# Loading q in runs of eight tokens, with the last tokens late, loads planned behind the transposes, and q @ kv joined with the next kv

## Chip, cores and metric

The kernel runs on one core of one Trainium2 chip. The metric is the device time of one execution in microseconds. A run counts as slow if it lies more than 1.5% above the fastest of the same kernel. Medians and ranges below are of all runs; ratios, intervals and verdicts (faster, same or slower at 2%, or unclear) are of fast runs. The sessions ran on several chips, so each kernel is compared with runs of the kernel before in the same session.

## The reference

A linear attention over 8 batches feeds a SoLU layer with a LayerNorm; B = 8, H = 8, S = 576, D = 64, d_model = 512, d_ff = 1024.

```python
kv  = np.einsum('bhsd,bhse->bhde', k, v)
o   = np.einsum('bhsd,bhde->bhse', q, kv)
x   = o / np.sqrt(np.mean(o * o, -1, keepdims=True) + 1e-6) * g_norm   # then to (B*S, H*D)
h   = x @ w_in
u   = h * softmax(h, -1)
ln  = (u - mean(u)) / np.sqrt(var(u) + 1e-6) * g_ln
out = ln @ w_out                                                      # (4608, 512), float32
```

## The kernel before

The tokens are worked off in nine chunks of 512. Chunks 0 to 7 are the first 512 tokens of each batch; the ninth holds the last 64 tokens of all eight. A small list scheduler (`Plan.order`) fixes the order of the pieces on each engine from estimated lengths. The output leaves in 36 tiles of 128 rows by 512 columns, four per chunk, with four output buffers (`ob`). GpSimd issues the loads; the SP queue issues most stores, and the DMA transposes of q for chunks 4 to 8.

```python
XBAR = tuple(range(4, NC))               # chunks whose q is transposed by DMA; NC = 9
bufs = {"k": 3, "v": 3, "q": 3, "qT": 3, ... "ob": 4}
q_last = big.tile([128, H, 4, D], BF16, name="q_last")
# ...
def load_q(b, hs):                       # 4 tokens in a run: 512 B packets after the cast to bf16
    nc.gpsimd.dma_start(
        T["q", b].rearrange("p h j d -> p h (j d)")[:, hs],
        q[b, :, 0:512, :].rearrange("h (p j) d -> p h (j d)", j=4)[:, hs])
# ...
def q_turn(c):
    t = T["qT", c] = tile_of(("qT", c), [128, H, 2, 128], BF16)
    nc.sync.dma_start_transpose(
        t.rearrange("q h y p -> q (h y) p"), T["q", c].rearrange("p h j d -> p (h j d)"))
# ...
def o_mm(c, hf, tag):                    # q @ kv; the last chunk takes every eighth column of each batch
    ...
            for b in [c] if c < B else range(B):
                cols = slice(0, 128) if c < B else slice(b, 128, B)
# ...
def store(c, m):
    j = 2 * (m % 2) + m // 2
    if c < B:                            # DRAM side: 128 rows x 512
        dst = out[c * S:c * S + 512, :].rearrange("(p j) d -> j p d", j=4)
    else:                                # DRAM side: 16 x 8 x 512
        dst = out.rearrange("(b s) d -> b s d", b=B)[:, 512:S, :].rearrange("b (p j) d -> j p b d", j=4)
    (nc.scalar if c == NC - 1 and m % 2 else nc.sync).dma_start(dst[j], T["ob", c, m][:, :])
```

The softmax here doesn't subtract the row's maximum and nothing guards it: scores larger than these inputs give would overflow.

## Time and profile before

| | before |
|---|---|
| time, median (range) | 197.0 us (196.5 to 197.7), 3 runs |
| span of the profiled run (whose own time is 195.0 us) | 193.1 us |
| TensorE busy | 179.8 us, 93% |
| a store of 256 KB, issue to landing | 2.9 us (median) |
| bytes stored | 9.44 MB |

The page's main lines are in the prediction below. Two of its other parts matter here: the chain of work that ended last (shares of the span by engine, then by line) and the DMA issues (count, KB each, us to landing).

```profile
PE 64%; DMA 20%; ACT 7%; POOL 4%; DVE 2%; issue 2%; SPq 0%; POOLq 0%; DVEq 0%; ACTq 0%
...
out_dram<-ob_sb SPq DMA_DIRECT2D x34, 256.0 KB, 2.9
```

The end is set by TensorE.

### The profile page before, as it was taken

The numbers are of one execution on the slowest core, as the hardware profiler recorded it, in microseconds if no ns is written. First come the engines' busy times: TensorE is split into PE (matmuls) and PEld (weight loads), VectorE is DVE, ScalarE is ACT, GpSimd is POOL, SyncE is SP. The second block draws the span as 40 slices with busy tenths as digits, with TensorE's granted clock in tenths as the row PEclk, the third lists the DMA queues.
The fourth block names the chain that finished last, engine by engine and source line by source line (L and its number), as shares of the span: only waits on it lengthen the run. The fifth ranks groups of instructions, "written<-read, shape, count | busy, mean of one in ns | idle before, by whom it ended". The sixth has DMA issues, their size and how long they took to land.

```text
span 193.1 us, 5442 instructions
## 1 busy us (share of the span) xinstructions
PE 179.8 (93%) x2282; PEld 88.3 (46%) x2282; DVE 122.6 (63%) x241; ACT 141.0 (73%) x245; POOL 127.9 (66%) x136
## 2 busy tenths in 40 slices
PE   7897997898899998999899999999999999999991
PEld 2352454553354643544354435445445554544460
DVE  1456588468684887496477658567575747666450
ACT  2038888869895997799689987989789496655520
POOL 7981799500999987977499776568285838846200
PEclk9999999999999999999999999999999999999999
DMA  1999999999996999899999996363111111211206
GB/s 22 204 204 266 357 203 205 206 224 248 233 201 86 147 190 258 113 185 168 292 214 200 212 111 182 108 116 114 54 54 58 58 54 58 109 58 54 110 7 213
DMA packets 36040, 29.71 MB, mean 154 GB/s; under 512 B 11816, under 2 KB 30512, under 8 KB 36016
## 3 DMA queue, kind: packets, MB, share of 16 engines
q0 software_dynamic: 20112, 17.30, 56.4%
q1 hardware_dynamic: 15616, 11.67, 22.4%
q10 hardware_dynamic: 288, 0.39, 0.6%
q8 instruction: 18, 0.29, 0.6%
q14 instruction: 6, 0.05, 0.1%
HBM read 32.51 MB, written 9.44 MB: 217 GB/s over the span
## 4 chain that ended last, share of the span: by engine, by line
PE 64%; DMA 20%; ACT 7%; POOL 4%; DVE 2%; issue 2%; SPq 0%; POOLq 0%; DVEq 0%; ACTq 0%
PE out_ps L582 26%; PE h_ps L468 24%; DMA w_out_f<-in_moe_w_out_dram 9%; DMA v_sb<-in_v_dram 7%; PE misc_ps L534 4%; DMA out_dram<-ob_sb 4%; PE s_ps L369 3%; PE o_ps L348 2%; ACT e_sb L476 2%; PE misc_ps L291 1%; DVE u_sb L483 1%; ACT osq_sb L363 1%; ACT rst_sb L377 1%; ACT lss_sb L373 1%; PE h_ps L592 1%
## 5 line engine op out<-in xcount | busy, mean ns | idle before, releaser
L468 PE MATMUL h_ps<-x_sb,w_in_sb 128*128 128x512 bf16 x276 | 70.3, 379 | 3.0 <-DVE u_sb L483 1.7
L582 PE MATMUL out_ps<-w_out_sb,u_sb 128*128 128x512 bf16 x272 | 69.0, 379 | 0.5 <-issue 0.5
L494 POOL TENSOR_TENSOR usq_sb<-u_sb 128x512 bf16<-128x512 bf16 x50 | 52.0, 1042 | 25.5 <-DVE u_sb L483 25.4
L483 DVE TENSOR_TENSOR u_sb<-h_ps,e_sb 128x512 bf16<-128x512 f32 x69 | 47.3, 688 | 30.4 <-ACT e_sb L476 29.5
L500 POOL TENSOR_TENSOR es_sb<-e_sb 128x512 bf16<-128x512 f32 x36 | 45.9, 1274 | 21.6 <-ACT e_sb L476 21.2
L476 ACT ACTIVATE e_sb<-h_ps,zero_t 128x512 f32<-128x512 f32 x69 | 47.1, 684 | 12.6 <-PE h_ps L468 11.8
L468 PEld LDWEIGHTS <-w_in_sb 128*128 128x128 bf16 x288 | 27.3, 98 | 37.5 <-issue 6.9
L582 PEld LDWEIGHTS <-u_sb 128*128 128x128 bf16 x280 | 26.1, 98 | 31.0 <-issue 2.0
L363 ACT ACTIVATE osq_sb<-o_ps,zero_t 128x512 bf16<-128x512 f32 x31 | 20.1, 683 | 15.3 <-PE o_ps L348 15.3
L614 DVE TENSOR_SCALAR ob_sb<-out_ps,rstd 128x512 f32<-128x512 f32 x33 | 24.6, 745 | 10.0 <-PE out_ps L582 4.3
L390 DVE SCALAR_TENSOR_TENSOR x_sb<-o_ps,g_rep,rst_sb 128x512 bf16<-128x512 f32 x32 | 23.9, 749 | 8.6 <-ACT rst_sb L377 8.4
L377 ACT ACTIVATE rst_sb<-lss_sb,zero_t 128x512 f32<-128x512 f32 x32 | 23.2, 726 | 0.7
L373 ACT ACTIVATE lss_sb<-s_ps,eps_t 128x512 f32<-128x512 f32 x32 | 22.0, 688 | 2.2 <-PE s_ps L369 2.2
L492 ACT ACTIVATE usq_sb<-u_sb,zero_t 128x512 bf16<-128x512 bf16 x22 | 15.8, 719 | 5.4 <-DVE u_sb L483 5.4
L369 PE MATMUL s_ps<-osq_sb,head_mean 128*128 128x512 bf16 x34 | 12.9, 380 | 0.3 <-ACT osq_sb L363 0.3
L534 PEld LDWEIGHTS <-stat_sel 128*32 128x32 bf16 x720 | 10.1, 97 | 3.8 <-issue 3.8
L217 POOL DMA_DIRECT2D k_sb<-in_k_dram x10 | 7.8, 784 | 4.3 <-DMA w_in_sb<-in_moe_w_in_dram 2.9
L198 PE MATMUL s_ps<-zeros 128*128 128x512 bf16 x28 | 9.2, 453 | 1.4 <-DVE zero_t L163 1.2
L225 POOL DMA_DIRECT2D q_sb<-in_q_dram x10 | 8.6, 856 | 2.5 <-DMA w_in_sb<-in_moe_w_in_dram 1.5
L348 PE MATMUL o_ps<-qT_sb,kvd 64*64 64x32 bf16 (+1 forms) x240 | 8.2, 256 | 1.1 <-DMA qT_sb<-q_sb 0.7
L291 PEld LDWEIGHTS <-k_sb 64*64 64x64 bf16 x576 | 6.7, 107 | 4.9 <-issue 4.9
L291 PE MATMUL misc_ps<-v_sb,k_sb 64*64 64x64 bf16 x360 | 7.6, 194 | 0.8 <-DMA v_sb<-in_v_dram 0.7
(85 smaller groups left out, 131.6 us busy)
## 6 DMA issues: line engine op xcount, KB each, us to landing
out_dram<-ob_sb SPq DMA_DIRECT2D x34, 256.0 KB, 2.9
k_sb<-in_k_dram POOLq DMA_DIRECT2D x6, 576.0 KB, 13.3
v_sb<-in_v_dram POOLq DMA_DIRECT2D x6, 576.0 KB, 14.3
q_sb<-in_q_dram POOLq DMA_DIRECT2D x6, 512.0 KB, 15.9
w_out_f<-in_moe_w_out_dram POOLq DMA_DIRECT2D x1, 2048.0 KB, 16.5
k_sb<-in_k_dram POOLq DMA_DIRECT2D x4, 288.0 KB, 11.5
v_sb<-in_v_dram POOLq DMA_DIRECT2D x4, 288.0 KB, 12.2
q_sb<-in_q_dram POOLq DMA_DIRECT2D x4, 256.0 KB, 12.2
```

The source lines that it names most:

```text
L363: nc.scalar.activation(out=t[:, :], in_=T[("o", *i)].rearrange("p a b c -> p (a b c)"), func=AF.Square, bias=zero_t[:, :])
L369: nc.tensor.matmul(t[:, :], head_mean[:, :], T["osq", i][:, :], start=True, stop=True)
L373: nc.scalar.activation(out=t[:, :], in_=T["s", i][:, :], func=AF.Ln, bias=eps_t[:, :])
L377: nc.scalar.activation(out=t.rearrange("p a b c -> p (a b c)"), in_=T["lss", i][:, :], func=AF.Exp, scale=-0.5, bias=zero_t[:, :])
L390: nc.vector.scalar_tensor_tensor(out=T["x", c][:, 2 * hf:2 * hf + 2, z], in0=T["o", c, hf, z][:, :, :, :], scalar=g_rep[:, :], in1=T["rst" ...
L468: nc.tensor.matmul(t[:, :], w_in_sb[:, dt, f * 128:(f + 1) * 128], T["x", c][:, dt].rearrange("p a b c -> p (a b c)"), start=(dt == 0), st ...
L476: nc.scalar.activation(out=T["e", c, f // 2][:, f % 2, :], in_=T["h", c, f][:, :], func=AF.Exp, bias=zero_t[:, :])
L483: nc.vector.tensor_tensor(out=T["u", c][:, f, :], in0=T["h", c, f][:, :], in1=T["e", c, f // 2][:, f % 2, :], op=MUL)
L494: nc.gpsimd.tensor_tensor(out=dst, in0=src, in1=src, op=MUL)
L500: nc.gpsimd.tensor_tensor(out=T["es", c][:, n, :], in0=e[:, 0, :], in1=e[:, 1, :], op=ADD)
L582: nc.tensor.matmul(T["acc", c, m][:, :], T["u", c][:, f, m * 128:(m + 1) * 128], w_out_sb[:, f, :], start=(f == 0), stop=(f == NF - 1),)
L614: nc.vector.tensor_scalar_mul(out=t[:, :], in0=T["acc", c, m][:, :], scalar1=T["rstd", c][:, m:m + 1])
```

## The change

The intent: q packets twice as long, cheaper contiguous columns in the last chunk, its loads moved to a quieter time, no loads in front of the DMA transposes, and one fewer change of TensorE's tiling mode in some chunks (q @ kv and kv run with the array split into tiles of 64x64, the large matmuls with the whole of 128x128; two neighbours of one mode save a change). A token is now one of nine in a run; tokens 0 to 7 of each run make up the chunk of a batch, and every ninth token goes to the last chunk. The core of the diff:

```diff
-    q_last = big.tile([128, H, 4, D], BF16, name="q_last")
+    q_last = big.tile([128, NP, B, D], BF16, name="q_last")
@@ loads of k, v and q: one function, 8 tokens in a run for q
+        js = 8 if name == "q" else 9
+            T[name, b].rearrange("p n j d -> p n (j d)")[:, hs.start // 2:hs.stop // 2],
+            src[b, hs].rearrange("(n r) (p j) d -> (r p) n (j d)", r=2, j=9)[:, :, 0:js * D],
     def load_q_last(b):
+        nc.gpsimd.dma_start(q_last[:, :, b, :], q[b].rearrange("(n r) (p j) d -> (r p) n j d", r=2, j=9)[:, :, 8, :])
@@ loads of chunk b wait in the plan for the transpose of chunk b-1
-        behind = ... [("h_mm", b - 3, 2 if b == 3 else 0)]
+        behind = ... [("h_mm", b - 3, 2 if b == 3 else 0)] + ([("turned", b - 1)] if b - 1 in XBAR else [])
-                 [("h_mm", 2 + b // 2, 4 * (b % 2))], load=0.5)          # q_last
+                 [("h_mm", 4 + b // 4, 2 * (b % 4))], load=0.7)
+            plan.add(("turned", c), "wait", 2.0, r - 0.05, lambda: None, [("q", c, 0)] if c < B else [])
@@ q @ kv of the last chunk
-            for b in [c] if c < B else range(B):
+            for y in [slice(0, 4)] if c < B else range(4):
...
-                            T["qT", c][rows, 4 * hf + 2 * pp + hh, :, cols], start=True, stop=True,
+                            T["qT", c][rows, n, y, 64 * hh:64 * hh + 64], start=True, stop=True,
@@ stores: the rows of a tile are now tokens 2y+z and 2y+z+2 of 64 runs
+    def rows_of(c, z, y):
+        if c < B:
+            return out[c * S:c * S + S, :].rearrange("(p j) d -> j p d", j=9)[2 * y + z:2 * y + z + 3:2]
+        return out.rearrange("(b p j) d -> j b p d", p=64, j=9)[8, 2 * y + z:2 * y + z + 3:2]
-        (nc.scalar if c == NC - 1 and m % 2 else nc.sync).dma_start(dst[j], T["ob", c, m][:, :])
+            rows_of(c, m // 2, 2 * (m % 2)), T["ob", c, m][:, :]
@@ joined pieces
+    for c in range(1, B - 3):
+        plan.fuse([("o_mm", c + 2, 1), ("kv_mm", c + 3, 0)], c + 1.1)
```

More of the change, by code (lines that the diff above doesn't have):

```diff
@@ L25, in __init__ @@
     def __init__(self, bufs):
-        self.pieces, self.users, self.bufs = {}, {}, bufs
+        self.pieces, self.users, self.bufs, self.names = {}, {}, bufs, {}
     def add(self, name, engine, length, rank, fn, needs=(), uses=(), first=(), load=0.0):
@@ L31, in add, with fuse @@
             self.users.setdefault(key, []).append(name)
+    def fuse(self, names, rank):
+        parts = [self.pieces.pop(n) for n in names]
+        self.names.update({n: names[0] for n in names})
+        self.pieces[names[0]] = (
+            "pe", sum(p[1] for p in parts), rank, lambda: [p[3]() for p in parts], sum([list(p[4]) for p in parts], []),
+            sum([list(p[5]) for p in parts], []), 0.0,
+        )
     def order(self):
+        for n, p in self.pieces.items():
+            self.pieces[n] = (*p[:4], sorted({self.names.get(m, m) for m in p[4]} - {n}, key=str), *p[5:])
+        self.users = {key: sorted({self.names.get(m, m) for m in u}, key=str) for key, u in self.users.items()}
         free, done, queue, lanes, mode = {}, {}, 2.5, [], {}
@@ L210, with load @@
     plan.add("ident", "pool", 1.0, -1.95, make_ident)
-    def load_kv(name, src, b, hs):
+    def load(name, src, b, hs):
+        js = 8 if name == "q" else 9
         if hs.start == 0:
-            T[name, b] = tile_of((name, b), [128, NP, 9, D], BF16)
+            T[name, b] = tile_of((name, b), [128, NP, js, D], BF16)
         nc.gpsimd.dma_start(
-            T[name, b].rearrange("p n i d -> p n (i d)")[:, hs.start // 2:hs.stop // 2],
-            src[b, hs].rearrange("(n r) (p i) d -> (r p) n (i d)", r=2, i=9),
-        )
-    def load_q(b, hs):
-        if hs.start == 0:
-            T["q", b] = tile_of(("q", b), [128, H, 4, D], BF16)
-        nc.gpsimd.dma_start(
-            T["q", b].rearrange("p h j d -> p h (j d)")[:, hs],
-            q[b, :, 0:512, :].rearrange("h (p j) d -> p h (j d)", j=4)[:, hs],
+            T[name, b].rearrange("p n j d -> p n (j d)")[:, hs.start // 2:hs.stop // 2],
+            src[b, hs].rearrange("(n r) (p j) d -> (r p) n (j d)", r=2, j=9)[:, :, 0:js * D],
         )
     def load_q_last(b):
-        nc.gpsimd.dma_start(
-            q_last[b:128:B].rearrange("p h j d -> p h (j d)"),
-            q[b, :, 512:S, :].rearrange("h (p j) d -> p h (j d)", j=4),
-        )
+        nc.gpsimd.dma_start(q_last[:, :, b, :], q[b].rearrange("(n r) (p j) d -> (r p) n j d", r=2, j=9)[:, :, 8, :])
     def load_w_in(half):
@@ L253 @@
         at = b - 9.0 if b > 1 else (-2.0, -1.5)[b]
-        behind = [] if b < 2 else [("h_mm", 0, 0)] if b == 2 else [("h_mm", b - 3, 2 if b == 3 else 0)]
+        behind = [] if b < 2 else [("h_mm", 0, 0)] if b == 2 else [("h_mm", b - 3, 2 if b == 3 else 0)] + ([("turned", b - 1)] if b - 1 in XBAR else [])
         for g, hs in enumerate(heads(b)):
@@ L257 @@
             n = len(heads(b))
-            for i, (name, src) in enumerate((("k", k), ("v", v))):
-                plan.add((name, b, g), "pool", 0.75 if n == 1 else 0.6, at + part + 0.01 * i,
-                         lambda name=name, src=src, b=b, hs=hs: load_kv(name, src, b, hs),
+            for i, (name, src) in enumerate((("k", k), ("v", v), ("q", q))):
+                plan.add((name, b, g), "pool", (0.8 if name == "q" else 0.75) if n == 1 else 0.6, at + part + (0.01 * i if i < 2 else 0.02 if b < 2 else 0.1),
+                         lambda name=name, src=src, b=b, hs=hs: load(name, src, b, hs),
                          behind, uses=[(name, b)] if g else [],
-                         first=[] if g else [(name, b)], load=2.9 / n if b < 3 else 3.5)
-            plan.add(("q", b, g), "pool", 0.9 if n == 1 else 0.7, at + part + (0.02 if b < 2 else 0.1),
-                     lambda b=b, hs=hs: load_q(b, hs), behind,
-                     uses=[("q", b)] if g else [], first=[] if g else [("q", b)], load=2.7 / n if b < 3 else 3.3)
-        plan.add(("q_last", b), "pool", 0.6, 2.0 + 0.5 * b, lambda b=b: load_q_last(b),
-                 [("h_mm", 2 + b // 2, 4 * (b % 2))], load=0.5)
+                         first=[] if g else [(name, b)], load=(2.55 if name == "q" else 2.9) / n if b < 3 else 3.2 if name == "q" else 3.5)
+        plan.add(("q_last", b), "pool", 0.7, 4.0 + 0.25 * b, lambda b=b: load_q_last(b),
+                 [("h_mm", 4 + b // 4, 2 * (b % 4))], load=0.7)
     for half in range(2):
@@ L313, in qT_mm @@
     def qT_mm(c, hf, tag):
-        t = T["qTp", c, hf] = bank((tag,), [128, 4, 2, 128], BF16)
-        for h in range(4):
-            for y in range(2):
-                src = T["q", c][:, 4 * hf + h, 2 * y:2 * y + 2, :].rearrange("p z d -> p (z d)")
-                nc.tensor.transpose(t[:, h, y, :], src, ident[:, :])
+        t = T["qTp", c, hf] = bank((tag,), [128, 2, 4, 128], BF16)
+        for n in range(2):
+            for y in range(4):
+                src = T["q", c][:, 2 * hf + n, 2 * y:2 * y + 2, :].rearrange("p z d -> p (z d)")
+                nc.tensor.transpose(t[:, n, y, :], src, ident[:, :])
     def qT_copy(c, hf):
         if hf == 0:
-            T["qT", c] = tile_of(("qT", c), [128, H, 2, 128], BF16)
-        dst, src = T["qT", c][:, 4 * hf:4 * hf + 4], T["qTp", c, hf][:, :, :, :]
+            T["qT", c] = tile_of(("qT", c), [128, NP, 4, 128], BF16)
+        dst, src = T["qT", c][:, 2 * hf:2 * hf + 2], T["qTp", c, hf][:, :, :, :]
         if c == 1:
@@ L330, in q_turn @@
     def q_turn(c):
-        t = T["qT", c] = tile_of(("qT", c), [128, H, 2, 128], BF16)
+        t = T["qT", c] = tile_of(("qT", c), [128, NP, 4, 128], BF16)
         nc.sync.dma_start_transpose(
-            t.rearrange("q h y p -> q (h y) p"), T["q", c].rearrange("p h j d -> p (h j d)")
+            t.rearrange("q n y p -> q (n y) p"), T["q", c].rearrange("p n j d -> p (n j d)")
         )
     def o_mm(c, hf, tag):
-        ts = [bank((tag,), [128, 2, 2, 128], FP32) for z in range(2)]
+        ts = [bank((tag,), [128, 2, 4, 64], FP32) for z in range(2)]
         for z in range(2):
@@ L342, in o_mm @@
         for pp in range(2):
-            for b in [c] if c < B else range(B):
-                cols = slice(0, 128) if c < B else slice(b, 128, B)
+            n = 2 * hf + pp
+            for y in [slice(0, 4)] if c < B else range(4):
                 for hh in range(2):
@@ L348, in o_mm @@
                         nc.tensor.matmul(
-                            ts[z][hh * 64:hh * 64 + 64, pp, :, cols], kvd[rows, b, hh ^ z, 2 * hf + pp, :],
-                            T["qT", c][rows, 4 * hf + 2 * pp + hh, :, cols], start=True, stop=True,
+                            ts[z][hh * 64:hh * 64 + 64, pp, y, :], kvd[rows, c if c < B else 2 * y + z, hh ^ z, n, :],
+                            T["qT", c][rows, n, y, 64 * hh:64 * hh + 64], start=True, stop=True,
                         )
@@ L375, in s_exp @@
     def s_exp(*i):
-        t = T["rst", i] = tile_of(("rst", i), [128, 2, 2, 128], FP32)
+        t = T["rst", i] = tile_of(("rst", i), [128, 2, 4, 64], FP32)
         nc.scalar.activation(
@@ L381, in s_rsqrt @@
     def s_rsqrt(*i):
-        t = T["rst", i] = tile_of(("rst", i), [128, 2, 2, 128], FP32)
+        t = T["rst", i] = tile_of(("rst", i), [128, 2, 4, 64], FP32)
         nc.scalar.activation(
@@ L388, in x_mul @@
         if (hf, z) == (0, 0):
-            T["x", c] = tile_of(("x", c), [128, NP, 2, 2, 128], BF16)
+            T["x", c] = tile_of(("x", c), [128, NP, 2, 4, 64], BF16)
         nc.vector.scalar_tensor_tensor(
@@ L429 @@
             kvs = [("kv", b, x, part) for b in ([c] if c < B else range(B)) for x in ((hf,) if b < 2 else range(2)) for part in range(3)]
-            plan.add(("o_mm", c, hf), "pe", 0.25 if c < B else 1.2, r + w * (0.35 + 0.5 * hf),
+            plan.add(("o_mm", c, hf), "pe", 0.25 if c < B else 0.6, r + w * (0.35 + 0.5 * hf),
                      lambda c=c, hf=hf, tag=tag: o_mm(c, hf, tag), [("qT", c) if c in XBAR else ("qT", c, hf), *kvs],
@@ L605, in store_cols @@
     def store_cols(x):
-        dst = out.rearrange("(b s) (x d) -> b s x d", b=B, x=2)[:, 512:S, x, :].rearrange("b (p j) d -> j p b d", j=4)[3]
-        (nc.sync, nc.scalar)[x].dma_start(dst, T["ob", NC - 1, 3][:, x])
+        cols = slice(x * d_model // 2, (x + 1) * d_model // 2)
+        (nc.sync, nc.scalar)[x].dma_start(
+            rows_of(NC - 1, 1, 2)[:, :, cols], T["ob", NC - 1, 3][:, x]
+        )
     def scale(c, m):
@@ L614, in scale @@
             nc.vector.tensor_scalar_mul(out=t[:, :], in0=T["acc", c, m][:, :], scalar1=T["rstd", c][:, m:m + 1])
+    def rows_of(c, z, y):
+        if c < B:
+            return out[c * S:c * S + S, :].rearrange("(p j) d -> j p d", j=9)[2 * y + z:2 * y + z + 3:2]
+        return out.rearrange("(b p j) d -> j b p d", p=64, j=9)[8, 2 * y + z:2 * y + z + 3:2]
     def store(c, m):
-        j = 2 * (m % 2) + m // 2
-        if c < B:
-            dst = out[c * S:c * S + 512, :].rearrange("(p j) d -> j p d", j=4)
-        else:
-            dst = out.rearrange("(b s) d -> b s d", b=B)[:, 512:S, :].rearrange("b (p j) d -> j p b d", j=4)
-        (nc.scalar if c == NC - 1 and m % 2 else nc.sync).dma_start(dst[j], T["ob", c, m][:, :])
+        (nc.scalar if c == NC - 1 and m % 2 else nc.sync).dma_start(
+            rows_of(c, m // 2, 2 * (m % 2)), T["ob", c, m][:, :]
+        )
     plan.add("w_mean", "pe", 2.0, -0.5, lambda: [w_mean(f) for f in range(NF)], ["w_out", "g_mean", ("o_mm", 0, 1)],
```

## The prediction

> **What bounds the kernel now.** I read the page's totals first, then the waits of TensorE and of the DMA queue, then the timeline of TensorE, then the DMA view in windows. The page:
>
> ```profile
> span 193.1 us, 5442 instructions
> PE 179.8 (93%) x2282; PEld 88.3 (46%) x2282; DVE 122.6 (63%) x241; ACT 141.0 (73%) x245; POOL 127.9 (66%) x136
> DMA  1999999999996999899999996363111111211206
> q0 software_dynamic: 20112, 17.30, 56.4%
> q1 hardware_dynamic: 15616, 11.67, 22.4%
> ```
>
> TensorE is busy 93% of the span. The DMA engines are nearly full until about 85 us and almost idle after 125 us (slices of 4.8 us). Up to 17.6 us TensorE only fills time with warming matmuls. After that the waits and the timeline show eleven gaps: 1.13, 0.90, 0.47, 0.72, 0.35, 0.90, 0.19, 0.20, 0.50, 0.67 and 0.37 us, together 6.4 us, the last at 97 us. From there to the end TensorE has no gap: only fewer or cheaper matmuls shorten that half. The two gaps near 95 us and their cause:
>
> ```profile
> PE o_ps L348 <- DMA qT_sb<-q_sb: 0.7, 1, 0.7
> DVE ob_sb L614 <- DMA out_dram<-ob_sb: 2.0, 1, 2.0
> ...
> 80.37 7.29 SPq L333 DMA_TRANSPOSE qT_sb<-q_sb  x1
> 87.76 3.44 SPq L623 DMA_DIRECT2D out_dram<-ob_sb  x4
> ```
>
> The second DMA transpose was issued at 80.37 us, just after the loads of the next chunk (78.4 to 80.9 us). It sat 7.29 us in its queue and landed after 14.5 us (the last one, with quiet engines, took 4.3); the stores behind it came late, VectorE waited 2.0 us for an output buffer and TensorE 0.67 and 0.37 us.
>
> **What the Trainium skill says.** (1) "TensorEngine Tiling (Array Packing)", Key Properties: changing the tiling mode drains TensorE. The trace agrees: a 4-matmul group takes 0.86 us, 0.97 after a tiled block, and the block starts 0.10 us late. (2) "DMA: Bandwidth & Descriptors", How many engines (k): a DMA is split over the largest k up to 16 that divides the slowest dimension, other than 1, of both of its access patterns; its rules for authors add that an outermost dimension of c under 16 confines the DMA to c engines. (3) Same page, Why a DMA increments its semaphore by 16: on the SP and ACT queues only the k engines used post a completion. The trace agrees with (2) and (3). In the first 10 us the SP queue moves two transfers of 64 rows and one of 8:
>
> ```profile
> q1 hardware_dynamic: 176, 0.00, 1.0%
> ```
>
> 176 is 64+16 twice and 8+8: the transfer with 8 rows closes with 8 packets, not 16. A window of 150 to 158 us with two stores of 128 rows shows 288 packets, 128+16 twice. (4) Same page, Specifications: about 27 GiB/s for one engine. The same window shows it for stores:
>
> ```profile
> GB/s 82 430 379 389 31 0 0 0 0 0 0 0 0 0 0 0 0 0 82 0 0 0 0 0 0 0 0 0 0 0 0 0 0 51 358 440 379 82 0 0
> ```
>
> One 256 KB store runs at about 400 GB/s over 16 engines, 25 GB/s each.
>
> **The change part by part.** *q in runs of eight tokens.* q packets grow from 512 B to 1 KB. The landings before give 2.62 us for a q of 512 KB and 2.95 us for a k or v of 576 KB with packets of 1152 B: both 200 GB/s. The packet size did not limit q, so I expect 0 to 0.1 us per chunk, 0.2 us in all.
>
> *Last tokens.* q @ kv of the last chunk is 2 x 64 matmuls of 64x32, on every eighth column; it becomes 2 x 32 of 64x64 on contiguous columns.
>
> ```profile
> 144.45 1.13 PE L348 MATMUL o_ps<-qT_sb,kvd 64*64 64x32 bf16 x64
> 154.29 1.14 PE L348 MATMUL o_ps<-qT_sb,kvd 64*64 64x32 bf16 x64
> ```
>
> Each group holds TensorE for 1.06 us, 16.6 ns a matmul. kv, 72 matmuls of 64x64 in 0.60 us, costs 8.3 ns each. 32 matmuls at 8.3 to 16.6 ns are 0.27 to 0.53 us; the saving is 0.5 to 0.8 us twice, centre 1.2 us, on the saturated half. The q_last loads become 8 x 512 packets of 128 B, issued after about 95 us; q @ kv of that chunk now needs them at about 147 us. Harmless.
>
> *One piece on TensorE.* The instruction order shows that two of the four pairs were adjacent already. The other two (at 103 and 123 us) save one change of mode each: q @ kv alone plus kv alone, with their switches, 0.44 + 0.82 us, against 1.03 us for the adjacent pair at 85 us, so 0.23 us each, 0.46 us.
>
> *Loads behind the transpose.* On GpSimd the loads of chunk 5 move back by one square and one sum (1.04 + 1.27 us), those of chunk 6 by about one square. The first transposes then run in emptier queues; both gaps at 95 us go (1.04 us), perhaps part of those at 67 to 73 us.
>
> Sum so far: 0.2 + 1.2 + 0.46 + 1.04 = 2.9 us, less some for new waits: 2.5 us, which is 194.5 us measured. This is what the change is meant to do.
>
> *What it does to the stores, unsaid.* A store of 128 rows was one pattern of 128 (the last chunk's 16 x 8). Now the 128 rows of a tile are tokens 2y+z and 2y+z+2 of 64 runs of nine: the built program carries 2 x 64 x 512, outermost 2, against 128 partitions. By (2) the common divisor is 2, so all 36 tiles' stores go through two engines. I take that at its word. One store: 256 KB over 2 x 25 GB/s is 5.2 us; 36 stores 189 us on those two engines, where before each engine had 9.44 MB / 400 GB/s = 24 us. The same two engines must carry their sixteenth of every load, and a load lands only when its slowest engine is done. From 38.7 us (first store) they have: stores 189 us; loads of q2 and of chunks 3 to 7, 2.6 + 5 x (2 x 2.95 + 2.6) = 45 us; transposes, the second queue's share, 22.4% of 193 = 43 us less 24 of stores, 20 us. Together 254 us, so an end at 38.7 + 254 = 293 us of span if nothing overlaps, and at 38.7 + 189 = 228 us if only the stores counted. Four output buffers hold about one chunk of stores, so nothing larger than that can be hidden: VectorE stops on ob, the out banks stay full, TensorE stops. Measured time is 3.9 us above the span (197.0 against 193.1). Between 232 and 297 I choose 280, nearer the upper end, because packets of several queues share an engine's time. The gains of 2.5 us vanish in this.
>
> **The rivals.** *A: sixteen engines after all.* The decoder may treat 2 x 64 as 128, or cut along the inner dimension. For it: a change with so much tuning in it would hardly be made at 280 us; against it: the 8 closing packets above. Then 194.5 us (193 to 197). *B: two engines, yet hidden.* Stores are asynchronous, and 4 x 5.2 = 21 us per chunk is close to a chunk's 17.8 us on TensorE (115.9 to 133.7 us). If the two engines could run above 25 GB/s, or read and write sides of loads and stores overlapped wholly, I get 36 stores at about 4.5 us, or 38.7 + 162 + 4 = 205 at the least, more likely 230. Nothing in the trace shows an engine above 27.5 GB/s (440/16). *C: the old schedule with new waits*: the joined pieces make q @ kv wait for the kv banks, or the transpose of the last tokens waits for small packets in front of the stores. Each would cost 1 to 2 us: 196 to 198 us.
>
> **Range and chances.** The outcome has two heaps. Two engines (B included): about 0.65, spread over 230 to 305, mostly 260 to 297. Sixteen engines: about 0.35 around 194.5, of which under 193.1 (faster by over 2%) 0.08, the rest within 2%. An 80% range must then take in most of both: 194 to 305; the point is the middle of the larger heap.
>
> **What would show it.** Two engines: the second queue's stores count 128+2 packets each instead of 128+16; stores land after 6 us or more instead of 2.9; GB/s falls to some 50 in the late slices; VectorE's ob waits for the store, tens of us in total, head the waits; the chain that ended last is mostly DMA out_dram. Sixteen engines: stores land in 3 us, packets stay 144 each. For the rest: the q @ kv rows of 64x64 near 0.3 to 0.5 us a group; no 7 us transpose issue; no gap at 95 us; q loads still at 200 GB/s. The prediction is wrong if stores of 2 x 64 rows land as fast as before, or if the two engines move far more than 27 GB/s each.

## The result, and the profile after

| | before | after |
|---|---|---|
| time, median (range) | 197.4 us (196.5 to 201.8), 4 runs | 293.0 us (292.6 to 293.7), 4 runs |
| ratio | | 1.487, interval 1.480 to 1.494 |
| span of the profiled run | 193.1 us | 290.9 us |
| TensorE busy | 93% | 67% |

One run of before, 201.8 us, is slow; the others are fast. A ratio here is the mean time of one kernel's fast runs over that of the other's in the same session, so it is not quite the ratio of the medians. The change makes the kernel slower by half.

The page of the kernel after:

```profile
span 290.9 us, 5312 instructions
PE 194.3 (67%) x2218; PEld 92.4 (32%) x2218; DVE 122.1 (42%) x241; ACT 142.4 (49%) x245; POOL 128.9 (44%) x136
...
GB/s 90 204 323 229 208 208 217 167 39 183 107 37 87 127 165 52 108 215 59 63 100 57 59 61 99 54 68 51 89 54 51 54 51 51 53 52 51 51 50 39
...
q1 hardware_dynamic: 15126, 11.67, 30.9%
...
DMA 72%; PE 12%; DVE 3%; POOL 2%; ACT 2%; issue 1%; DVEq 0%; POOLq 0%
DMA out_dram<-ob_sb 58%; DMA qT_sb<-q_sb 7%; DMA qT_sb<-q_last 5%; PE h_ps L469 5%; PE out_ps L583 3%; DMA v_sb<-in_v_dram 2%; DVE ob_sb L617 1%; DVE u_sb L484 1%; POOL k_sb L230 1%; DVE w_out_sb L574 1%; PE misc_ps L210 1%; PE out_ps L568 1%; PE s_ps L368 1%; PE o_ps L469 1%; PE o_ps L347 1%
```

Three things to see. The second queue (q1) carries the same 11.67 MB in fewer packets. Before it had 15616 = 176 + 35 x 144 + 5 x 2080: the first 10 us, 35 transfers of output on this queue with 128 data packets and 16 closing ones (one from each engine used, point 3 of the prediction), five transposes. Now 15126 = 176 + 35 x 130 + 5 x 2080: only two closing packets for each output transfer, hence two DMA engines. The throughput falls to a floor of 51 GB/s, about 25.6 for each of two engines. And the chain that ended last, 64% TensorE before, is 72% DMA, most of it stores.

The waits of the engines (us in total, times, longest):

```profile
DVE ob_sb L617 <- DMA out_dram<-ob_sb: 65.9, 19, 7.6
...
PE o_ps L347 <- DMA qT_sb<-q_sb: 26.2, 3, 15.8
```

VectorE waited 2.0 us for an output buffer before, once; now 65.9 us in 19 waits. TensorE waited 0.7 us for a transposed q; now 26.2, and 6.5 more for that of the last tokens, 32.7 in four places. The timeline of the SP queue shows why the second wait follows from the stores (start, us, what was issued):

```profile
98.82 22.17 SPq L332 DMA_TRANSPOSE qT_sb<-q_sb  x1
121.09 12.49 SPq L627 DMA_DIRECT2D out_dram<-ob_sb  x3
133.69 15.94 SPq L332 DMA_TRANSPOSE qT_sb<-q_sb  x1
```

A transpose of q takes 16 to 22 us to issue (that of the last tokens 13.3) where it took up to 7.29 us. The Trainium skill, "DMA: Bandwidth & Descriptors", section Queues, rings and completion order, says that SP owns one ring on each engine and that an engine consumes a ring's descriptors in order: the transpose's share on the two busy engines lies behind the stores. The trace agrees as far as these times go.

The end of the span in windows (busy us of PE, PEld, DVE, ACT and POOL with their instructions, then granted clock, DMA share, GB/s):

```profile
240.00:260.00 20.00, 13.26 (x136) 7.18 (x134) 5.28 (x12) 3.91 (x7) 3.24 (x3) 0.91 0.14 52
260.00:280.00 20.00, 0.00 (x0) 0.00 (x0) 0.48 (x1) 1.16 (x2) 0.00 (x0) 0.50 0.13 51
280.00:291.00 11.00, 0.00 (x0) 0.00 (x0) 0.00 (x0) 0.00 (x0) 0.00 (x0) 0.50 0.11 42
```

TensorE has finished before 260 us; over the last 30 us only stores are left, at the two engines' rate. The granted clock reads 0.50 where TensorE is idle (0.853 in the mean over the span, and 406 instead of 379 ns for a matmul of h). I take it for a consequence of the waits, since the chain that ended last is 72% DMA and 12% TensorE; no run tests it alone.

### The profile page after: what moved, and what is told of

Same layout as the page of the kernel before. It is cut to its first block, busy times and chain, and to the rows that moved or that the text cites. A ratio compares the mean times of both kernels' runs of the same rounds, so it can differ in the third digit from the quotient of the medians.

```text
span 290.9 us, 5312 instructions
## 1 busy us (share of the span) xinstructions
PE 194.3 (67%) x2218; PEld 92.4 (32%) x2218; DVE 122.1 (42%) x241; ACT 142.4 (49%) x245; POOL 128.9 (44%) x136
## 3 DMA queue, kind: packets, MB, share of 16 engines
q1 hardware_dynamic: 15126, 11.67, 30.9%
## 4 chain that ended last, share of the span: by engine, by line
DMA 72%; PE 12%; DVE 3%; POOL 2%; ACT 2%; issue 1%; DVEq 0%; POOLq 0%
DMA out_dram<-ob_sb 58%; DMA qT_sb<-q_sb 7%; DMA qT_sb<-q_last 5%; PE h_ps L469 5%; PE out_ps L583 3%; DMA v_sb<-in_v_dram 2%; DVE ob_sb L617 1%; DVE u_sb L484 1%; POOL k_sb L230 1%; DVE w_out_sb L574 1%; PE misc_ps L210 1%; PE out_ps L568 1%; PE s_ps L368 1%; PE o_ps L469 1%; PE o_ps L347 1%
## 5 line engine op out<-in xcount | busy, mean ns | idle before, releaser
L469 PE MATMUL h_ps<-x_sb,w_in_sb 128*128 128x512 bf16 x276 | 76.9, 406 | 12.0 <-DVE u_sb L484 10.5
L583 PE MATMUL out_ps<-w_out_sb,u_sb 128*128 128x512 bf16 x272 | 74.5, 398 | 8.5 <-DVE ob_sb L617 5.3
L469 PEld LDWEIGHTS <-w_in_sb 128*128 128x128 bf16 x288 | 28.3, 102 | 54.8 <-issue 28.9
L583 PEld LDWEIGHTS <-u_sb 128*128 128x128 bf16 x280 | 27.4, 101 | 43.7 <-issue 12.8
L347 PE MATMUL o_ps<-qT_sb,kvd 64*64 64x256 bf16 (+1 forms) x176 | 8.2, 270 | 34.8 <-DMA qT_sb<-q_sb 26.2
L347 PEld LDWEIGHTS <-kvd 64*64 64x64 bf16 x192 | 3.9, 115 | 42.8 <-issue 22.7
L368 PE MATMUL s_ps<-osq_sb,head_mean 128*128 128x512 bf16 x34 | 13.9, 409 | 3.7 <-ACT kvd L310 2.6
L535 PEld LDWEIGHTS <-stat_sel 128*32 128x32 bf16 x720 | 11.4, 104 | 4.2 <-issue 4.2
L230 POOL DMA_DIRECT2D q_sb<-in_q_dram x10 | 7.5, 751 | 2.8 <-DMA w_in_sb<-in_moe_w_in_dram 1.4
L290 PEld LDWEIGHTS <-k_sb 64*64 64x64 bf16 x576 | 7.4, 107 | 2.3 <-issue 2.3
```

Source lines behind the costliest of these rows:

```text
L230: nc.gpsimd.dma_start(T[name, b].rearrange("p n j d -> p n (j d)")[:, hs.start // 2:hs.stop // 2], src[b, hs].rearrange("(n r) (p j) d -> ...
L469: nc.tensor.matmul(t[:, :], w_in_sb[:, dt, f * 128:(f + 1) * 128], T["x", c][:, dt].rearrange("p a b c -> p (a b c)"), start=(dt == 0), st ...
L583: nc.tensor.matmul(T["acc", c, m][:, :], T["u", c][:, f, m * 128:(m + 1) * 128], w_out_sb[:, f, :], start=(f == 0), stop=(f == NF - 1),)
```

## The experiments

**Theory:** stores on two engines make the whole difference. **Rivals:** the transposes' lateness is what sets the end; the two-level pattern itself is slow whatever the number of engines; the new addresses of a tile's rows are slow to write; the new loads or the new order of pieces cost the time.

### 1. The kernel after, each store as two transfers of 64 rows

```diff
-            rows_of(c, m // 2, 2 * (m % 2)), T["ob", c, m][:, :]
+        for i in range(2):
+                ...                      # the same dma_start, now inside the loop
+                rows_of(c, m // 2, 2 * (m % 2))[i], T["ob", c, m][64 * i:64 * i + 64, :]
```

Each transfer is now 64 x 512 on both sides. The two column halves of the last tile are split alike.

> The changed kernel, each store of 128 rows cut into two of 64 rows, so that the outermost dimension is 64 on both sides and sixteen engines carry it. Same rows, same addresses, same strides. Two-engine theory: the whole loss goes and the planned gains remain, 194.5 us (193 to 197), 128+32 packets a tile. Rival 1 (the addresses: rows 18 KB apart are slow to write): still over 280 us. Rival 2 (the other parts of the change, order of loads and joined pieces, cost the time): still over 250 us.

Measured: 192.83 us median (192.28 to 195.97, 7 runs), before 195.63 in the same session; ratio 0.988, interval 0.981 to 0.995 (verdict unclear: whether it is faster than before by 2% is open; that the 100 us are gone is not). Two of the seven runs are slow, the profiled one among them. The result is correct. Its page and DMA issues:

```profile
q1 hardware_dynamic: 16176, 11.68, 27.5%
...
out_dram<-ob_sb SPq DMA_DIRECT2D x68, 128.0 KB, 3.2
```

16176 = 176 + 70 x 80 + 5 x 2080: 64 data and 16 closing packets for each transfer, so all sixteen engines. Everything else of the change is still there, and 100 us are gone. The rivals that blame the loads, the order of pieces or the addresses of the rows, which are the same, fall.

### 2. The kernel before with stores on two, four and eight engines

The reverse. The rows of a tile are taken in another order, so that the DRAM side has an outermost dimension of 2, 4 or 8 against the same 128 partitions; bytes, rows, packets and instructions stay. The rows land in wrong places, so the result is wrong.

```diff
-            dst = out[c * S:c * S + 512, :].rearrange("(p j) d -> j p d", j=4)
+            dst = out[c * S:c * S + 512, :].rearrange("(p w j) d -> j w p d", j=4, w=2)   # or w=4, w=8
```

> The kernel before with one change: the stores of chunks 0 to 7 are written as 2 x 64 x 512 (every second row of the same 128 rows; rows come out permuted, so the result is wrong on purpose). Two-engine theory, summed as in the prediction: 32 stores x 5.2 = 167 us on two engines, plus 45 us of loads and 20 us of transposes after 38.7 us: a span of about 271 us, 265 to 278 measured. Rival (other parts of the change cost the time): 197 us.

> As the run with 2 x 64, but 4 x 32 x 512 (result permuted, wrong on purpose): four engines. 32 stores x 2.6 = 84 us on four engines. While loads run, one chunk costs these engines 8.5 us of loads, 4 of transposes and 10.4 of stores, 23 us against 17.8 us on TensorE, so about 5 us lost on each of four chunks: 210 to 220 us. After the loads end the stores fit (10.4 against 17.8 us) and nothing more is lost. Rival (only the case of two engines is bad, or the shape of the pattern itself is slow): under 200 us, or as slow as with two.

> The kernel before with the stores of chunks 0 to 7 as 8 x 16 x 512, eight engines by the rule of common divisors; wrong results on purpose, as with 2 and 4. Eight engines at 25 to 26 GB/s move a store in 1.3 us and all 32 of them in 40 us; with a half share of the 45 us of loads no longer in the way beyond that (each engine: 40 us of stores, 45 us of loads, 20 us of transposes, 105 us within the 154 us after 38.7 us), the work fits beside TensorE: the theory says 195.5 to 199 us, ratio 1.00 to 1.015, 128+8 packets a store, 15360 packets in the second queue. If something else than the engine count were at work (the pattern's two levels, say), it would stay above 205 us.

| outermost x rows | engines | time, us | closing packets a store (q1) |
|---|---|---|---|
| 128 (before) | 16 | 195.6 and 196.6 medians of the two sessions (fast runs 194.9 and 196.1 in the mean) | 16 (15616) |
| 8 x 16 | 8 | 202.2 median (198.4 to 206.9, 6 runs, two of them fast) | 8 (15360) |
| 4 x 32 | 4 | 214.0 median (212.9 to 215.0, 4 runs), ratio 1.097, interval 1.088 to 1.106 (recorded as unclear) | 4 (15232) |
| 2 x 64 | 2 | 275.3, one run, its state unknown | 2 (15168) |

The old kernel with stores of 2 x 64 shows the picture of the new one. Its waits:

```profile
DVE ob_sb L614 <- DMA out_dram<-ob_sb: 69.3, 19, 8.6
PE o_ps L348 <- DMA qT_sb<-q_sb: 25.7, 2, 14.5
```

The waits with four engines, then with eight:

```profile
PE o_ps L348 <- DMA qT_sb<-q_sb: 13.2, 3, 5.0
DVE ob_sb L614 <- DMA out_dram<-ob_sb: 7.0, 1, 7.0
```

```profile
PE o_ps L348 <- DMA qT_sb<-q_sb: 5.1, 2, 3.7
```

The time follows the number of engines. That two levels as such do not cost is seen best in experiment 5, where a two-level store of 64 x 2 rows has sixteen engines and lands in 2.4 us. With two, stores set the end: 38.7 + 32 x 5.2 + 45 + 20 = 270 us by the prediction's sum (the last chunk's four stores keep sixteen engines), and the span is 273.5. With four, the same sum gives 38.7 + 32 x 2.6 + 65 = 187 us, less than the 193.1 of before, yet the span is 212.6: now the sum no longer binds, and 13.2 of the 19.5 us by which the span grew stand in TensorE's waits for transposes. With eight I expected 195.5 to 199; the two fast runs gave 198.4 and 200.5 (1.7% above the fast runs of before in the mean, too few), the others up to 206.9. Eight was not free in these: TensorE waits 5.1 us for transposes, near the 5.7 us by which the span grew against the first profile of before.

### 3. The kernel after with all transposes on TensorE

```diff
-    XBAR = tuple(range(4, NC))
+    XBAR = ()
```

The stores keep two engines; no transpose passes through the DMA queues. With `XBAR` empty the rule that plans loads behind a transpose goes too, and TensorE and VectorE do the transposes' work.

> The changed kernel with every transpose of q on TensorE, none by DMA; the stores stay at 2 x 64. In the changed kernel TensorE waits about 50 us in four places for transposes that stand behind stores. If the two engines' time simply adds up, the 20 us of transposes go from 290 and about 270 us remain, now with the waits on output buffers. If the waits for transposes set the end by themselves, about 240 us.

Measured: 280.74 us, one run, span 279.0. Waits, and the chain that ended last:

```profile
DVE ob_sb L617 <- DMA out_dram<-ob_sb: 63.2, 17, 7.8
```

```profile
DMA 75%; PE 9%; DVE 4%; ACT 2%; POOL 2%; issue 1%; DVEq 0%; POOLq 0%
```

TensorE's waits for DMA transposes are gone, which is 32.7 us (the "about 50" of the expectation counts the weight loads' waits for the same transposes on top), and the end moves by 12 us only. So they did not set it: the rival that the late transposes set the end (240 us) falls. Removing 20 us of the two engines' work should have given 273 of span by the sum; 279.0 is 6 us above it. The transposes' work was partly hidden, or the sum's other terms are a few us short; I did not separate these.

### 4. The rest of the change, with the stores repaired

A control, then one part taken out at a time, 5 rounds on one chip.

> The same kernel as in split64 (stores of 64 rows), as the control on this chip for the three others. 192.3 to 193 us in its fast runs; in some runs 195.6 to 196, when the third DMA transpose meets the loads of the last chunk and TensorE waits 3 us for it.

Without the joined pieces (`plan.fuse(...)` deleted):

> Stores of 64 rows, without the joined piece on TensorE. By the prediction joining saves 0.46 us (two changes of mode): 0.3 to 0.7 us slower than the control. Rival (joining delays kv or q @ kv as much as it saves): equal or faster.

Without the loads planned behind the transpose:

```diff
-  ... + ([("turned", b - 1)] if b - 1 in XBAR else [])
```

> Stores of 64 rows, without the loads planned behind the transpose. By the prediction that part is worth 1.0 us: 0.7 to 1.5 us slower than the control in fast runs, with a transpose issue of 7 us and a TensorE wait for qT. Rival (the race goes on in both): equal, with as many slow runs.

With the planned distance tripled (`("turned", c), "wait", 2.0` becomes 6.0):

> Stores of 64 rows, and the planned wait behind a transpose raised from 2 to 6 us, so that the loads of chunks 5 to 7 are issued later. If the slow runs of the control come from loads issued just ahead of a transpose, all runs are now at 192 to 193 us and no transpose takes over 9 us to land. Rival (the loads then come too late, or the slow runs have another cause): slower than the control, or slow runs as before.

| kernel | median (range), us | mean of fast runs | ratio to before | slow runs |
|---|---|---|---|---|
| control | 195.69 (192.96 to 198.70) | 193.82 | 0.991 | 3 of 6 |
| not joined | 193.26 (192.74 to 197.38) | 193.00 | 0.988 | 2 of 6 |
| not behind the transpose | 193.02 (192.64 to 193.47) | 193.05 | 0.988 | 0 of 6 |
| distance 6.0 | 194.11 (193.70 to 195.34) | 194.29 | 0.994 | 0 of 6 |

The runs of before on the same chip had a median of 196.12 us (fast runs 195.49 in the mean, 4 of 11 slow). By fast runs alone the control is 0.8 us slower than either kernel with a part taken out. Three fast runs make up its mean, and one of 195.38 us makes the difference; without that run it is 193.04. So neither joining nor planning the loads behind the transpose is worth anything that I can measure here. What the second does is to make a race: the third transpose and the loads of chunk 7 become due in the same quarter of a microsecond. The profiled run of the first repaired kernel (experiment 1) was a slow one; its timeline of the two issuing engines:

```profile
95.85 0.75 POOL L230 DMA_DIRECT2D k_sb<-in_k_dram  x1
96.10 7.82 SPq L332 DMA_TRANSPOSE qT_sb<-q_sb  x1
```

The same in the profile of the kernel that is not joined, a fast run:

```profile
95.86 1.66 SPq L332 DMA_TRANSPOSE qT_sb<-q_sb  x1
96.08 0.81 POOL L230 DMA_DIRECT2D k_sb<-in_k_dram  x1
```

Where the load is issued 0.25 us ahead, the transpose takes 7.82 us to issue, lands after 16.6 us, and TensorE waits 3.1 us for it; where it is issued 0.22 us behind, 1.66 us. The control's profile, slow too, shows the first picture again (7.81 us, 3.3 us of waiting). The order of issue fits beyond these: in the five profiles of repaired kernels where a k load goes out 0.22 to 0.42 us ahead of a transpose, all seven such transposes take 7.57 to 8.33 us. With the distance of 6.0 all transposes are quick (at most 2.2 us) and no run is slow, but loads come later and it is 1.2 us slower than the version without any such rule; that the late loads are why was not tested. That every slow run has the cause of the two profiled ones is not shown. The slow runs of experiments 1 and 4 are of two sorts: 195.6 to 196.3 us at a mean clock of 0.997 or 0.998, as both profiled ones, and 197.3 to 198.7 us at 0.982 to 0.990, none of them profiled. And before, without any such rule, had slow runs in every session.

### 5. The best version again, and a store that needs no splitting

> Control, the version that was fast in all its runs, on a new chip session: stores cut in two, loads not planned behind the transposes, joined pieces kept. Expected 193.0 us (192.6 to 193.5), ratio 0.985 to 0.993, no slow run. If slow runs come back here (195 to 198 us), the reading that the race between the third transpose and the loads of the last chunk makes them is wrong.

> As the control, and without the joined pieces. If joining saves 0.46 us as predicted, this run is 0.3 to 0.6 us slower than the control of the same call; if the joined pairs come out adjacent anyway or the saving drowns, within 0.3 us. After the earlier run without joining I expect the latter: 193.0 us.

In the third kernel TensorE reads x with the two tokens of a pair side by side, so the rows of a tile come out in the order of DRAM: 64 runs of two tokens, outermost 64, one transfer per tile.

```diff
-                t[:, :], w_in_sb[...], T["x", c][:, dt].rearrange("p a b c -> p (a b c)"),
+                t[:, :], w_in_sb[...], T["x", c][:, dt].rearrange("p z (t y) c -> p (z t) c y", y=2),
-            return out[c * S:c * S + S, :].rearrange("(p j) d -> j p d", j=9)[2 * y + z:2 * y + z + 3:2]
+            return out[c * S:c * S + S, :].rearrange("(p j) d -> p j d", j=9)[:, 2 * y + z:2 * y + z + 3:2]
```

The loads are not planned behind the transposes, as in the control, and the last chunk's stores are changed alike.

> As the control, but each store stays one transfer: x is read by TensorE with its two tokens of a pair side by side (a pattern of 4 x 64 x 2 with a step of 64 inside), so that the rows of a tile lie in DRAM as 64 runs of two tokens. The outermost dimension is then 64 against 128 partitions and the theory of common divisors says 16 engines: 128+16 packets a store, stores landing in about 3 us, no output buffer waits. If TensorE reads such a pattern at full rate, h stays at 379 ns a matmul and the time is 193 us (192.5 to 194). If the stepped read halves its rate, 276 matmuls of 379 ns grow by up to 0.2 us each: 55 us more, 230 to 250 us. If the split needs the outermost dimensions to be equal, stores stay on fewer engines and the time goes above 200 us.

| kernel | median (range), us | ratio to before | slow runs |
|---|---|---|---|
| split, not behind the transpose | 193.00 (192.44 to 193.57) | 0.990, interval 0.985 to 0.994 | 0 of 6 |
| the same, not joined | 193.31 (193.02 to 205.13) | 0.992, interval 0.987 to 0.997 | 1 of 6 |
| one store of 64 x 2 rows | 264.38 (264.34 to 264.88) | 1.357 | 0 of 6 |

Before had 195.99 (fast runs 194.98 in the mean). The first line repeats experiment 4: twelve runs of this version in two sessions, none slow, 1.0 to 1.25% ahead of the fast runs of before. It is the best that I have. Without joining, 0.37 us slower in the mean of fast runs (193.35 against 192.98), which is near the predicted 0.46 but within the scatter of 1.1 us; in experiment 4 the joined kernel was the slower one. In the profiles of these two kernels TensorE is busy for 178.4 us joined and 179.2 not joined, yet both spans are 191.3 us. The one run of 205.13 has no profile and stays unexplained.

The third line is a trade. The costliest group and the DMA issues of its page:

```profile
q1 hardware_dynamic: 15616, 11.67, 15.3%
...
L469 PE MATMUL h_ps<-x_sb,w_in_sb 128*128 128x512 bf16 x276 | 143.8, 645 | 0.7 <-DVE x_sb L389 0.6
...
out_dram<-ob_sb SPq DMA_DIRECT2D x34, 256.0 KB, 2.4
```

As the theory said, an outermost 64 against 128 partitions gives sixteen engines: 15616 packets, as before the change, and stores that land in 2.4 us. But the stepped read costs TensorE 645 instead of 379 ns a matmul: 288 matmuls (276 in this group, 12 more into PSUM banks named o and out) x 0.266 us = 76.6 us, against 71.4 us measured over the control. I had expected at most 0.2 us each, and at most 250 us in all. The Trainium skill, "SBUF — State Buffer", section Door 1: The DMA port swizzle, has a note on 16-byte lines: a bf16 access may step by up to 8 elements for free. Here every second element is 64 away, 128 bytes, and the trace agrees that it is not free.

## Why the prediction was right, and where it was off

- **Which way, and why: right.** The step "by the common divisor, two engines" held: 130 packets a store, 51 GB/s, VectorE's 65.9 us for output buffers ahead of every other wait for a DMA, a chain of stores. (The landing time of a store, another sign named, is not in the trace of after.) Experiments 1 and 2 show it as the cause in both directions; rival A (sixteen engines after all) and rival B (two, but hidden) are out.
- **How much: 280 predicted, 293.0 measured**, inside the range, which says little, as 194 to 305 took in both outcomes. The sum of the two engines' work (254 us after the first store) was the better number: the first store was issued at 39.05 us, the span ended at 290.9, so 252 us. The term that was mis-sized was the discount from 297 to 280. None of it was due here. That 254 and 252 lie so close is in part luck: taking out the sum's 20 us of transposes moved the end by 12 (experiment 3), and the same sum is 3.5 us short in experiment 2 and 6 us short in experiment 3. The 3.9 us from span to time were misread: 193.1 and 197.0 belong to different executions. The profiled run itself took 194.98 us, and in every run with both, the time is 1.7 to 2.0 us above the span.
- **An engine's rate: right.** 25 GB/s assumed, about 25.6 measured (51 to 52 GB/s over two engines, 240 to 280 us).
- **Stores behind stores; what was not in it.** "The out banks stay full, TensorE stops" was the path that I named; TensorE's waits on that path, for VectorE to empty an out bank, are 5.3 us in two places. I did not foresee that transposes would stick in the SP rings for 13 to 22 us and stop TensorE for 32.7 us. Taking them off the DMA queues gained 12 us (experiment 3, one run), because the end belonged to the stores.
- **The last tokens: right for the group.** 0.5 to 0.8 us saved twice. In the best version a group holds TensorE for 0.38 us (145.14 to 145.52), where it was 1.06: twice 0.68 is 1.36 us. No run takes this part out alone, so its share of the gain in time is argued, not shown: TensorE's busy time fell from 179.8 to 178.4 us, but to 179.2 only where the pieces are not joined.
- **q in runs of eight: in line, not isolated.** Little was expected, 0.2 us. Between 24 and 36 us, where the loads fill the queues, before moves 203 to 208 GB/s and the best version 204 to 209.
- **Loads behind the transpose, 1.04 us: wrong.** The step "both gaps at 95 us go" attributed them to the order of issue. With the rule the first two did go out in 1.7 and 3.3 us, but the third took 7.8 us and TensorE waited 3.1 us for it (experiment 1). Without it the first two transposes take 7.9 and 8.1 us to issue (before: 1.7 and 7.3) and yet TensorE never waits for them:

```profile
61.11 7.93 SPq L332 DMA_TRANSPOSE qT_sb<-q_sb  x1
78.06 8.11 SPq L332 DMA_TRANSPOSE qT_sb<-q_sb  x1
```

  This is the SP timeline of the best version (the session of experiment 5). The second starts 2.3 us earlier than the 80.37 of before, and TensorE came 0.67 us too early there; by that arithmetic it lands in time. What moved it up I did not separate. The rule gains nothing that I can measure, and with it (at the distance of the change) 7 of 19 runs were slow, without it 1 of 18.
- **Joined pieces, 0.46 us: not confirmed.** A loss of 0.8 us and a gain of 0.37 us in two comparisons of fast runs, neither beyond the scatter. In the profile of either unjoined kernel three pairs stood apart, not two as counted in before.
- **The sum of gains: 2.5 us predicted, about 2.0 us** (194.98 less 192.98, means of fast runs of the session of experiment 5; 1.2 to 2.8 us by the interval) with the stores repaired and without the rule for loads. What is beyond the 1.36 us of the last tokens is not assigned to a part.

## What to carry to other kernels

When a change alters which rows a tile holds, look at the access pattern of its stores before anything else: a transfer with 128 rows as 2 x 64 has every byte and every data packet that it had, and one eighth of the engines. Count the closing packets of a transfer in the profile (128 + 16 against 128 + 2); that tells the number of engines without any timing. Cut such a transfer along its short outer dimension: two transfers of 64 rows brought 293 us back to 193, while reordering the compute to suit one transfer moved the cost to TensorE (264 us).

## What the Trainium skill lacked or had wrong

- "DMA: Bandwidth & Descriptors", How many engines (k): nothing wrong. Its rule held for outermost 2, 4, 8, 64 and 128 against 128 partitions (closing packets 2, 4, 8, 16, 16). It has no example of a 2 x 64 row store, which is what one meets; the price here was 275 us (2), 214 us (4) and 198.4 and 200.5 us (8, two fast runs) against 195 to 196 in the mean of fast runs.
- The same page, Specifications: about 27 GiB/s (29 GB/s) an engine is given; stores here ran at 25.6 GB/s an engine, with two of them busy to the end.
- The same page, DMA Transpose (X-bar): no time for a transpose beside other transfers. Here its issue took 1.6 to 1.7 us at best, 7.6 to 8.3 us with a load issued 0.2 to 0.4 us ahead, and 13 to 22 us in the kernel after, behind stores confined to two engines.
- "TensorEngine Tiling (Array Packing)", Key Properties: says that a change of mode drains, not what it costs. Joining two neighbours of one mode, estimated at 0.23 us each from the trace, gained -0.8 and 0.37 us for three of them, within the scatter.
- "SBUF — State Buffer": says that a long step is penalised, without a size for TensorE. A matmul with 512 moving bf16 columns, alternating by 128 bytes, took 645 instead of 379 ns.
